# Transposing a long-convolution filter by halves, so that its first transform step shares the row-tiled code of the other inputs

## The chip, the cores and the metric

One core of one Trainium2 chip. The metric is the device time of one execution, in microseconds. The kernel before: 1922.31 us, median of 3 runs (1921.58 to 1922.76).

## The reference, cut to what matters

The reference is a forward pass and its gradients, for one sequence of 2048 steps of 1024 channels. It adds a gated MLP (three weight matrices of 1024 x 3584, with their gradients) to a convolution branch:

```python
kv = k_shift * v                                   # 4-tap shift of k, times v
y  = irfft(rfft(kv_pad) * rfft(ssm_k_pad))[:S]     # long convolution, one filter per channel
y  = q * (y + kv * ssm_D)
out = x + y + MLP(layernorm(x))                    # and the gradients of all inputs but B_x
```

`ssm_k`, the filter, has shape (channels, time); every other input of the convolution has shape (time, channels). So the filter alone must be transposed before it is transformed.

## The kernel before

The MLP's large matmuls keep TensorE busy. The convolution, in 8 groups of 128 channels, is cut into small steps; each is issued after 8 or 16 large matmuls. `hn` is one group's filter, 128 channels x 2048 time steps. Sixteen whole transposes turn it into `hT`. In each of them the filter's columns are the weights: they are loaded into TensorE first (`PEld`, `LDWEIGHTS <-hn` in the profile), and an identity matrix of 128 columns is then streamed past them (`MATMUL pst<-ident,hn`). With time written as 32 q' + 16 u + r, row 2q' + u of `hT` holds the steps with that q' and u: even rows are u = 0, odd rows u = 1.

```python
def h_tile(self, st):
    hT = self.ttile("hT")
    hv = st["hn"][:].rearrange("p r c -> p (r c)").rearrange("p (q r) -> p r q", r=16)
    pst = self.ps.tile([P, 16, P], BF16, name="pst", tag="aps")
    for r in range(16):
        self.pri.now()
        self.pri.pin(self.nc.tensor.transpose(pst[:, r, :], hv[:, r, :], self.identA[:]))
    self.act(hT[:, 0:16, :], pst[:])
    return hT
```

The first step of the filter's transform needs the rows of one u only. The table `RH` therefore has two versions, each zero in the rows of the other u, and the step makes four passes of two 128-row matmuls:

```python
def fwd1_filter(self, st, hT):
    B = st["Bh"] = self.big.tile([P, 64, NB1, 2], BF16, name="B", tag="big")
    for r0 in range(0, NB1, 8):
        ps = self.ps.tile([P, 1024], F32, name="ps0", tag="aps")
        for jj in range(2):
            r = r0 % 16 + 4 * jj
            self.mm(ps[:, 512 * jj:512 * jj + 512], self.RH[:, r0 // 16].rearrange("p e a l -> p (e a l)"),
                    hT[:, r:r + 4, :].rearrange("p r c -> p (r c)"))
        self.act(B[:, :, r0:r0 + 8, :], ps[:].rearrange("p (r cp i) -> p cp r i", r=8, i=2))
        yield
```

The other inputs are loaded with u = 0 on partitions 0 to 63 and u = 1 on 64 to 127. Their first step uses 64-row matmuls, two at a time on the two halves of TensorE's rows:

```python
def fwd1(self, st, key, src):
    ...
            ps = self.ps.tile([P, 2, 4, P], F32, name="ps1", tag="aps")
            for u in range(2):
                rows = slice(64 * u, 64 * u + 64)
                self.mm(ps[:, u].rearrange("p r c -> p (r c)"), self.R[rows].rearrange("p e a l -> p (e a l)"),
                        src[rows, j:j + 4, :].rearrange("p r c -> p (r c)"))
    ...
```

## Time and profile before

| | before |
|---|---|
| time, median of 3 | 1922.31 us |
| span of the profiled run | 1918.5 us |
| TensorE busy | 1909.4 us |
| VectorE, ScalarE busy | 47%, 33% of the span |
| filter transposes, per group, from the end of the block before to the next block | 1.01 us |
| first step of the filter, per group | 4 x 0.431 = 1.72 us |

TensorE is busy nearly without a gap. A step of the convolution branch thus costs what it delays the large matmul behind it, and this is read in the timeline from start to start, not from the durations. TensorE's waits (engine, tile, line, what it waited for; total us, times, longest):

```profile
PE ps_g L805 <- DMA wg<-in_B_W_gate_dram: 1.6, 1, 1.6
PE ps_warm L851 <- POOL warm L848: 1.5, 1, 1.5
PE ps_g L805 <- DVE xnT L839: 1.0, 2, 0.7
```

All of them lie in the first 104 us of 1918.

### The profile page before, as it was taken

How to read it: one execution, taken by the hardware profiler on the slowest of the kernel's cores; microseconds unless marked ns; L12 is line 12 of the kernel's file. 1: busy time of each engine (PE TensorE's matmuls, PEld its weight loads, DVE VectorE, ACT ScalarE, POOL GpSimd, SP SyncE). 2: the span in 40 equal slices, each digit the busy share in tenths (PEclk: the TensorE clock that was granted, in tenths of full speed). 3: DMA queues.
4: the chain of work that ended last, by engine and by line, in shares of the span. 5: the costliest groups of instructions: out<-in, count | busy, mean ns of one | idle time of the engine just before them, and what ended most of it. 6: DMA issues, size and time to landing. Idle time of an engine off the chain costs nothing.

```text
span 1918.5 us, 36320 instructions
## 1 busy us (share of the span) xinstructions
PE 1909.4 (100%) x15582; PEld 886.9 (46%) x15582; DVE 910.2 (47%) x1364; ACT 635.8 (33%) x867; POOL 15.7 (1%) x38
## 2 busy tenths in 40 slices
PE   9999999999999999999999999999999999999999
PEld 4444444444444444444444444444444544444444
DVE  6767767767777754534444354310122232222222
ACT  5854354364364354354344344321000000000000
POOL 1100000000000000000000000000000000000000
PEclk9999999999999999999999999999999999999999
DMA  9975778974874982645663633385999964554553
GB/s 249 276 179 144 178 185 183 221 189 133 186 187 134 248 225 78 175 128 183 158 163 92 170 100 122 100 203 209 257 240 254 235 157 121 121 121 121 121 121 72
DMA packets 628002, 323.16 MB, mean 168 GB/s; under 512 B 458360, under 2 KB 597376, under 8 KB 627840
## 3 DMA queue, kind: packets, MB, share of 16 engines
q1 hardware_dynamic: 617344, 299.99, 64.1%
q10 hardware_dynamic: 9216, 16.65, 2.9%
q0 software_dynamic: 1280, 4.20, 0.7%
q8 instruction: 122, 2.00, 0.4%
q14 instruction: 40, 0.33, 0.1%
HBM read 143.79 MB, written 95.44 MB: 125 GB/s over the span
## 4 chain that ended last, share of the span: by engine, by line
PE 96%; DVE 1%; ACT 1%; DMA 1%; issue 0%; POOL 0%; SPq 0%; ACTq 0%; POOLq 0%
PE ps_x L1283 20%; PE ps_w L1056 20%; PE ps_o L1214 10%; PE ps_h L805 9%; PE ps_u L805 9%; PE ps_g L805 9%; PE ps_d L1056 9%; PE ps L72 7%; PE ps_d L1069 1%; PE ps_w L1069 1%; ACT ln_j L743 1%; PE ps_warm L851 0%; PE pst L308 0%; PE ps_r L1244 0%; DMA wg<-in_B_W_gate_dram 0%
## 5 line engine op out<-in xcount | busy, mean ns | idle before, releaser
L1056 PE MATMUL ps_w<-ugs,xn_nat 128*128 128x512 bf16 x1728 | 383.9, 379 | 0.0
L805 PEld LDWEIGHTS <-xnT 128*128 128x128 bf16 x1792 | 170.2, 98 | 212.0 <-issue 10.2
L1056 PEld LDWEIGHTS <-xn_nat 128*128 128x128 bf16 x1728 | 164.9, 98 | 199.4 <-issue 5.5
L805 PE MATMUL ps_g<-wg,xnT 128*128 128x512 bf16 x896 | 207.0, 379 | 3.2 <-DMA wg<-in_B_W_gate_dram 1.6
L1301 ACT ACTIVATE w<-xn,m 128x512 f32<-128x512 bf16 x32 | 24.3, 806 | 553.0 <-issue 317.2
L805 PE MATMUL ps_u<-wu,xnT 128*128 128x512 bf16 x896 | 207.0, 379 | 0.5 <-ACT gh L975 0.4
L805 PE MATMUL ps_h<-wdT,goT 128*128 128x512 bf16 x896 | 206.1, 379 | 0.0
L1283 PE MATMUL ps_x<-wgT,ggT 128*128 128x512 bf16 x896 | 198.6, 379 | 0.0
L1283 PE MATMUL ps_x<-wuT,guT 128*128 128x512 bf16 x896 | 198.6, 379 | 0.0
L1214 PE MATMUL ps_o<-wd,hT 128*128 128x512 bf16 (+1 forms) x896 | 187.6, 372 | 0.0
L1056 PE MATMUL ps_d<-g_nat,hs 128*128 128x512 bf16 x768 | 172.1, 379 | 0.0
L1283 PEld LDWEIGHTS <-guT 128*128 128x128 bf16 x896 | 87.7, 98 | 105.7
L1283 PEld LDWEIGHTS <-ggT 128*128 128x128 bf16 x896 | 87.7, 98 | 105.5
L1214 PEld LDWEIGHTS <-hT 128*128 128x128 bf16 x896 | 87.7, 98 | 99.9
L805 PEld LDWEIGHTS <-goT 128*128 128x128 bf16 x896 | 85.2, 98 | 102.6 <-issue 2.9
L319 DVE STREAM_TRANSPOSE flp<-C 128x1024 f32<-128x1024 f32 x48 | 90.5, 1930 | 83.4 <-ACT C L76 83.4
L908 DVE SCALAR_TENSOR_TENSOR ru<-ru,ps_u 128x512 bf16<-128x512 bf16 x112 | 76.5, 683 | 108.6 <-issue 43.3
L975 ACT CAST gh<-ps_h 128x512 bf16<-128x512 f32 x112 | 65.4, 585 | 164.1 <-PE ps_h L805 154.8
L1160 ACT CAST wi<-ps_w 128x512 bf16<-128x512 f32 x108 | 63.6, 589 | 161.8 <-PE ps_w L1056 150.1
L76 ACT CAST C<-ps 128x1024 bf16<-128x1024 f32 x96 | 92.5, 1015 | 69.1 <-PE ps L72 68.1
L319 DVE STREAM_TRANSPOSE flp<-B 128x1024 f32<-128x1024 f32 x48 | 90.8, 1939 | 48.6 <-ACT B L76 48.6
L1056 PEld LDWEIGHTS <-hs 128*128 128x128 bf16 x768 | 72.7, 98 | 88.9 <-issue 4.2
(175 smaller groups left out, 1482.6 us busy)
## 6 DMA issues: line engine op xcount, KB each, us to landing
ug_d<-ru SPq DMA_DIRECT2D x112, 256.0 KB, 3.6
ugs<-ug_d SPq DMA_DIRECT2D x112, 256.0 KB, 4.4
wg<-in_B_W_gate_dram SPq DMA_DIRECT2D x56, 256.0 KB, 4.7
wu<-in_B_W_up_dram SPq DMA_DIRECT2D x56, 256.0 KB, 4.8
h_d<-ht SPq DMA_DIRECT2D x112, 128.0 KB, 3.6
hs<-h_d SPq DMA_DIRECT2D x56, 256.0 KB, 5.1
out_dram<-wi SPq DMA_DIRECT2D x56, 256.0 KB, 2.5
gt<-in_grad_out_dram SPq DMA_DIRECT2D x32, 256.0 KB, 4.0
```

What stands on the lines that cost most here:

```text
L72: self.pri.pin(self.nc.tensor.matmul(out, lhsT=lhsT, rhs=rhs, start=start, stop=stop))
L76: self.pri.pin(self.nc.scalar.copy(out=out, in_=in_))
L319: self.pri.pin(self.nc.vector.transpose(out=df[:, c0:c0 + 32, :], in_=sf[:, c0:c0 + 32, :]))
L805: self.pri.pin(self.nc.tensor.matmul(ps[:], lhsT=xT[:, kt * P:(kt + 1) * P], rhs=w(kt), start=(kt == 0), stop=(kt == self.DT - 1)), always ...
L908: self.pri.pin(nc.vector.scalar_tensor_tensor(out=ru[s][:, 1, :], in0=ru[s][:, 0, :], scalar=0.0, in1=ps[:], op0=ALU.is_gt, op1=ALU.mult))
L975: self.pri.pin(nc.scalar.copy(out=gh[:], in_=ps[:]))
L1056: self.pri.pin(self.nc.tensor.matmul(ps[:], lhsT=lhsT(st), rhs=rhs(st), start=(st == 0), stop=(st == self.ST - 1)))
L1069: self.pri.pin(self.nc.tensor.matmul(ps[i][:], lhsT=lhsT(i, st), rhs=rhs(i, st), start=(st == 0), stop=(st == self.ST - 1)))
L1160: self.pri.pin(nc.scalar.copy(out=wo[0][:, d, :], in_=ps[:]))
L1214: nc.tensor.matmul(ps, lhsT=hT[:, kt, :], rhs=self.wd[:, kt, oc], start=(kt == 0), stop=(kt == self.FT - 1))
L1283: nc.tensor.matmul(ps, lhsT=T[:, kt, :], rhs=W[:, kt, oc], start=(i == 0), stop=(i == n - 1))
L1301: nc.scalar.activation(out=w[:, oc], in_=xn[:, oc], func=ACT.Identity, scale=m[:, 7:8], bias=m[:, 6:7])
```

## The change

The intent: put the filter on partitions in the layout of the other inputs (u = 0 below, u = 1 above), so that it can use their row-tiled first step. That step needs half the passes, and the zero-padded tables go. The price is 32 transposes of 64 columns in place of 16 of 128. (The removal of `RH` and of the two index vectors for it from the tables is cut here.)

```diff
     def h_tile(self, st):
         hT = self.ttile("hT")
-        hv = st["hn"][:].rearrange("p r c -> p (r c)").rearrange("p (q r) -> p r q", r=16)
+        hv = st["hn"][:].rearrange("p r c -> p (r c)").rearrange("p (q u r) -> p u r q", u=2, r=16)
         pst = self.ps.tile([P, 16, P], BF16, name="pst", tag="aps")
         for r in range(16):
-            self.pri.now()
-            self.pri.pin(self.nc.tensor.transpose(pst[:, r, :], hv[:, r, :], self.identA[:]))
+            for u in range(2):
+                self.pri.now()
+                self.pri.pin(self.nc.tensor.transpose(pst[64 * u:64 * u + 64, r, :], hv[:, u, r, :], self.identA[:]))
         self.act(hT[:, 0:16, :], pst[:])
...
-    def fwd1_filter(self, st, hT):
-        ...
...
-        f1h = self.fwd1_filter(st, hT)
+        f1h = self.fwd1(st, "Bh", hT)
         f1g = self.fwd1(st, "Bg", gt)
         yield f1h, (lambda: self.gate_grad(st)) if gi == 0 else None
-        yield f1h, tk
-        yield f1h, self.both(lambda: self.add_D(st), tk)
+        yield None, tk
         yield f1h, tk
         yield None, tk
-        flH = self.flip(st, "fH", st["Bh"][:])
+        yield None, self.both(lambda: self.add_D(st), tk)
+        flH = self.flip(st, "fH", st["Bh"][:].rearrange("p cp u r i -> p cp (u r) i"))
```

More of the change, by code (lines that the diff above doesn't have):

```diff
@@ L122, in tables @@
         self.R = con.tile([P, 2, 2, NB1], BF16, name="R")
-        self.RH = con.tile([P, 2, 2, 2, NB1], BF16, name="RH")
         self.RB = con.tile([P, 64], BF16, name="RB")
@@ L147, in tables @@
         n1 = pbit(63, 1.0, "n1p")
-        n1h = pbit(126, 0.5, "n1h")
-        up = pbit(1, 1.0, "up")
         def first(n, name):
@@ L160, in first @@
             return tr
-        tr = first(n1h, "H")
-        nup = lin(up, -1.0, 1.0, "nup")
-        for u, mu in ((0, nup), (1, up)):
-            V.tensor_scalar(out=self.RH[:, u], in0=tr[:], scalar1=mu[:], scalar2=None, op0=ALU.mult)
         tr = first(n1, "R")
@@ L320, in flip @@
             yield
-    def fwd1_filter(self, st, hT):
-        B = st["Bh"] = self.big.tile([P, 64, NB1, 2], BF16, name="B", tag="big")
-        for r0 in range(0, NB1, 8):
-            ps = self.ps.tile([P, 1024], F32, name="ps0", tag="aps")
-            for jj in range(2):
-                r = r0 % 16 + 4 * jj
-                self.mm(ps[:, 512 * jj:512 * jj + 512], self.RH[:, r0 // 16].rearrange("p e a l -> p (e a l)"),
-                        hT[:, r:r + 4, :].rearrange("p r c -> p (r c)"))
-            self.act(B[:, :, r0:r0 + 8, :], ps[:].rearrange("p (r cp i) -> p cp r i", r=8, i=2))
-            yield
     def add_D(self, st):
         for rows in (slice(0, 32), slice(64, 96)):
-            b0 = st["Bh"][rows, :, 0, :]
+            b0 = st["Bh"][rows, :, 0, 0, :]
             self.tt(b0, b0, st["sD"][rows].rearrange("p (cp i) -> p cp i", i=2), ALU.add)
```

## The prediction

> **What bounds the kernel now.** I read the page's busy shares and its chain first, then the sum of TensorE's waits, then the timeline of TensorE around the places that change.
>
> ```profile
> span 1918.5 us, 36320 instructions
> PE 1909.4 (100%) x15582; PEld 886.9 (46%) x15582; DVE 910.2 (47%) x1364; ACT 635.8 (33%) x867; POOL 15.7 (1%) x38
> PE 96%; DVE 1%; ACT 1%; DMA 1%; issue 0%; POOL 0%; SPq 0%; ACTq 0%; POOLq 0%
> ```
>
> TensorE is busy for 1909.4 of 1918.5 us and holds 96% of the chain that ends last. Its waits in the whole run come to 5.0 us (1.6 for a weight DMA, 1.5 at the start, the rest under 1). No other engine passes half. So the span is, nearly one for one, the sum of how long each step holds TensorE, and what the change is worth is the change of that sum. Busy figures of a group cannot be used for it: a record lasts longer than the time after which the next may start (a 512-column matmul is shown with 379 ns, yet 64 of them take 13.83 us from the first start to the start of what follows, 216 ns each). I therefore count from start to start.
>
> The convolution branch is fed to TensorE in small steps between blocks of 8 or 16 large matmuls. Timeline of TensorE at the end of one channel group and the start of the next (start, duration, instruction):
>
> ```profile
> 234.75 1.17 PE L308 MATMUL pst<-ident,hn 128*128 128x128 bf16 x16
> 235.76 1.89 PE L805 MATMUL ps_g<-wg,xnT 128*128 128x512 bf16 x8
> ...
> 245.33 0.59 PE L72 MATMUL ps<-hT,RH 128*128 128x512 bf16 x2
> 245.76 1.89 PE L805 MATMUL ps_h<-wdT,goT 128*128 128x512 bf16 x8
> 247.49 0.59 PE L72 MATMUL ps<-hT,RH 128*128 128x512 bf16 x2
> 247.92 1.89 PE L805 MATMUL ps_g<-wg,xnT 128*128 128x512 bf16 x8
> ...
> 252.24 3.62 PE L805 MATMUL ps_u<-wu,xnT 128*128 128x512 bf16 x16
> 255.79 0.61 PE L72 MATMUL ps<-gt,R 64*128 64x512 bf16 x4
> 256.32 3.63 PE L805 MATMUL ps_h<-wdT,goT 128*128 128x512 bf16 x16
> ```
>
> Line 308 is the filter's transpose, RH its zero-padded first step, and `gt,R` the first step of another input, which already is what the filter's will become. No line shows an idle gap: each step simply adds its length to the kernel.
>
> **What the Trainium skill says.** (1) "TensorEngine Tiling (Array Packing)", Key Properties: row or column tiles work independently, and changing the tiling mode drains the engine. The trace agrees: the four 64-row matmuls of `gt,R` start in two pairs, 0.54 us in all where four whole passes would take 0.86, and there is about 0.1 us lost before them and 0.1 after. (2) "TensorE: Matmul & The Clock Gate", Weight-path perf modes: the fast weight load needs 128 weights; the transposes fall to 64. The trace agrees that there is a difference: contiguous loads of 128 columns take 98 ns, those of 64 columns (RB) 110. (3) "SBUF — State Buffer", Door 1: lines of 16 bytes, and each access that crosses into a new line pays a penalty. The filter's weights are read with a step of 16 elements (32 bytes), so every element is on a new line; the change makes the step 32, again one line each. The trace shows the penalty:
>
> ```profile
> L308 PEld LDWEIGHTS <-hn x128: 142/148/164, 94.0 to 1116.4; 128*128 128x128 bf16 x128
> L837 PEld LDWEIGHTS <-ln_x x64: 95/98/98, 9.4 to 41.9; 128*128 128x128 bf16 x64
> ```
>
> The same transpose with contiguous weights (second line) loads in 98 ns and repeats every 56 ns; the strided one loads in 148 and repeats every 63 (1.01 us over 16), so here the load, not the matmul, sets the pace. (4) "PSUM — Partial Sum Buffer", PSUM bank collisions: two row tiles must not write one bank at the same time. The code that the filter now shares gives each half its own bank, so no wait comes of that.
>
> **The change part by part.**
>
> *First step of the filter.* Removed, per group: four steps of two matmuls, 245.76 − 245.33 = 0.43 us each (twice 216 ns, no drain), so 1.72 us. Added: two steps of four 64-row matmuls. From the timeline: the block before starts at 252.24 and holds 16 x 0.216 = 3.46 us, so it is through at 255.70; what follows the step starts at 256.32; the step costs 0.62 us. Two make 1.24. (A group at 1133 us, in the other phase of the kernel, gives 0.62 too.) Gain 0.48 us per group, 8 groups: 3.8 us. A naive count, eight passes made four, would be 0.86 per group; the entry into the tiled mode and the way out eat nearly half.
>
> *Transposes.* Removed per group: 16 of 128 columns, 235.76 − 234.75 = 1.01 us. Added: 32 of 64 columns, in pairs into the two halves of the partitions. Each still streams the 128-column identity. If the two of a pair run together, the floor is 16 pairs x 56 ns = 0.90 us, plus entry and exit of the mode. The nearest relative in the trace is the tap sums:
>
> ```profile
> 192.97 3.62 PE L805 MATMUL ps_u<-wu,xnT 128*128 128x512 bf16 x16
> 196.52 1.08 PE L72 MATMUL ps<-kp,gks 128*32 128x128 bf16 x64
> 197.53 3.63 PE L805 MATMUL ps_h<-wdT,goT 128*128 128x512 bf16 x16
> ```
>
> 64 matmuls with 32 weight columns each: the same number of weight columns (2048), and the same 16 rounds of 128 columns. The block before is through at 196.43, so the step costs 1.10 us: 0.90 and 0.20 of mode change. With contiguous weights I would thus write +0.1 us per group. With strided ones I have three readings of the 63 ns: if all reads of a partition share one rate (128 in 63 ns), a pair still reads 128 elements, costs 63 ns, and the step 16 x 0.063 + 0.2 = 1.2 us (+0.2 per group, +1.6 in all); if the strided load is now only an ordinary one without the fast mode, 64 columns are under the matmul's 56 ns and the step is 1.1 us (+0.8 in all); if the 63 ns belong to four streams of 32 elements side by side, a 64-column load in one stream takes twice that, 126 ns, and the step is 16 x 0.126 + 0.2 = 2.2 us (+1.2 per group, +9.7 in all). I hold the first two together at about 60%.
>
> *Evictions.* ScalarE's casts into B take 1006 to 1032 ns in both layouts (96 of them, one median of 1013), and there are four per group before and after; the copy of hT stays one of 1.87 us. Two casts now follow each other as they do for `gt`, where no wait of TensorE appears. The step counter of the branch advances equally often, so the interleaving stays.
>
> *Tables.* RH goes: on VectorE two casts of 0.28 us, three index steps and a few one-column instructions, on ScalarE one 0.40 us sine, all near 63 to 68 us. TensorE waits for none of them, so 0, with perhaps 0.4 us either way because ScalarE's order near 92 us, where one 0.4 us wait stands, can change.
>
> *Group 0.* Its third filter step is followed by the 1.6 us weight wait. What is gained or lost before that wait may partly be swallowed: 0.3 us at most, left out.
>
> *Sum.* −3.8 + 0.8 to 1.6 = −2 to −3 us in the likely case, −3.8 + 9.7 = +6 in the bad one.
>
> **The rivals.** (a) *The transposes give it all back* (the third reading above): for it speaks that the strided load already sets the pace, and that without the fast mode fewer streams may read; against it, that halving the columns halves the reads of each load, and that the four tiles of the tap sums load side by side without hurting. It makes about 1928 us. If also the two halves of a pair took turns, 32 x 0.126 + 0.2 = 4.2 us per group, +26 − 3.8: about 1944, still within 2%. (b) *The naive gain*: eight passes become four at full worth and nothing is lost on the transposes, −6.9 us, 1915 us. The 0.62 us of the existing step speaks against it. (c) *A new wait for evictions*: two PSUM tiles of a step must be emptied, about 2 us of ScalarE, before the branch's next use of them. The empty slot after each filter step leaves 3.5 us, and `gt` shows no wait with the same spacing, so 0; if it were to come, under 1 us per group and 8 in all. (d) *VectorE*: adding D moves two slots later, nearer to the flip of B. VectorE has gaps of over 1 us there, and TensorE's next use of the flip lies more than 4 us behind it. 0.
>
> **How the range and the chances follow.** Before is 1922.3 (1921.6 to 1922.8). The likely case gives 1919.5 to 1920.3, the bad one 1928.3. Weighing these at 60 and 30%, with the rest for the turns-taking and the naive cases, I set the middle at 1921 us, a little above the likely case, and the range at 1918 to 1930, which holds both main cases. A change of over 2% would need 38 us, that is 4.8 us per group on steps that now last 1.01 + 1.72 us. Faster: under 1%. Slower: 1%, if the strided loads without the fast mode are much worse than all readings here. Within 2%: 98%.
>
> **What would show each step right or wrong.** The filter's first step should appear as two steps of four 64-row matmuls, 0.60 to 0.65 us from the end of the block before to the start of the one after. The transposes should appear as 32 instructions with 64 weight columns; their step, 1.1 to 1.2 us if I am right, 2.2 if rival (a) is, and the weight load of hn near 110 to 150 ns or near 210. The sum of TensorE's waits should stay near 5 us. I am wrong if the span moves without these steps moving, if the transposes' step passes 1.5 us, or if a new waiting line of TensorE for a B or hT eviction appears.

## The result, and the profile after

| | before | changed |
|---|---|---|
| time, median of 4 runs each | 1921.94 us (1919.28 to 1922.76) | 1922.08 us (1921.57 to 1923.71) |
| span of the profiled run | 1918.5 us | 1919.8 us |
| transposes, per group | 1.01 us | 2.02 us |
| first step of the filter, per group | 1.72 us | 2 x 0.633 = 1.27 us |

The ratio is 1.0005, 95% interval 0.9987 to 1.0022: the same time. Here and below, a ratio is the mean time of one kernel's fast runs over that of the other's of the same rounds, so it is not quite the ratio of the medians quoted. "Us by the ratio" means the ratio minus one, times the median of before.

The page of the changed kernel, its head and the chain that ended last:

```profile
span 1919.8 us, 36326 instructions
PE 1891.6 (99%) x15472; PEld 886.3 (46%) x15710; DVE 908.9 (47%) x1354; ACT 633.6 (33%) x865; POOL 14.9 (1%) x37
PE 97%; issue 1%; DMA 1%; DVE 1%; ACT 0%; SPq 0%; DVEq 0%; ACTq 0%
```

TensorE's busy time seems to have fallen by 18 us. It has not: this trace has 15710 weight loads but only 15472 matmuls, so 238 matmul records are missing, and the page shows the holes as "issue". I read the timeline from a second profile of the same kernel (experiment 6), which has all 15710. End of one group and start of the next (start, duration, instruction):

```profile
230.55 3.62 PE L788 MATMUL ps_h<-wdT,goT 128*128 128x512 bf16 x16
234.09 2.00 PE L302 MATMUL pst<-ident,hn 128*64 128x128 bf16 x32
236.02 1.90 PE L788 MATMUL ps_g<-wg,xnT 128*128 128x512 bf16 x8
...
243.87 1.89 PE L788 MATMUL ps_h<-wdT,goT 128*128 128x512 bf16 x8
245.70 0.60 PE L72 MATMUL ps<-hT,R 64*128 64x512 bf16 x4
246.23 1.90 PE L788 MATMUL ps_h<-wdT,goT 128*128 128x512 bf16 x8
247.97 1.89 PE L788 MATMUL ps_g<-wg,xnT 128*128 128x512 bf16 x8
249.79 0.60 PE L72 MATMUL ps<-hT,R 64*128 64x512 bf16 x4
250.33 1.90 PE L788 MATMUL ps_g<-wg,xnT 128*128 128x512 bf16 x8
```

The 16 large matmuls from 230.55 hold TensorE for 16 x 0.216 = 3.46 us, to 234.01; the next block starts at 236.02. So the transposes cost 2.01 us. The block of 8 from 243.87 is through at 245.60, and the next starts at 246.23: 0.63 us for half of the first step. Over all groups the medians are 2.02 and 0.633 us.

The first line explains the transposes, in the same profile (durations in ns: least, median, most):

```profile
L302 PEld LDWEIGHTS <-hn x256: 185/204/209, 94.7 to 1120.1; 128*64 128x64 bf16 x128
L302 PE MATMUL pst<-ident,hn x256: 273/274/323, 94.8 to 1120.2; 128*64 128x128 bf16 x128
```

Half as many columns, and the load takes longer than the whole one of before (204 ns against 148). In the trace the two loads of a pair start 4 ns apart and the pairs repeat every 111 ns; a whole transpose repeated every 63 to 64. Per group the change gives back 1.724 - 1.266 = 0.46 us and takes 2.02 - 1.01 = 1.01: a loss of 0.55 us, 4.4 us in 8 groups. The timed runs show less than that. The experiments are about both points: why the halves are slow, and where the rest of the loss is.

### The profile page after: what moved, and what is told of

It is laid out like the page before. It is cut to its first block, busy times and chain, and to the rows that moved or that the text cites. A ratio compares the mean times of both kernels' runs of the same rounds, so it can differ in the third digit from the quotient of the medians.

```text
span 1919.8 us, 36326 instructions
## 1 busy us (share of the span) xinstructions
PE 1891.6 (99%) x15472; PEld 886.3 (46%) x15710; DVE 908.9 (47%) x1354; ACT 633.6 (33%) x865; POOL 14.9 (1%) x37
## 3 DMA queue, kind: packets, MB, share of 16 engines
q8 instruction: 123, 2.02, 0.4%
## 4 chain that ended last, share of the span: by engine, by line
PE 97%; issue 1%; DMA 1%; DVE 1%; ACT 0%; SPq 0%; DVEq 0%; ACTq 0%
PE ps_x L1266 20%; PE ps_w L1039 19%; PE ps_h L788 10%; PE ps_g L788 10%; PE ps_u L788 10%; PE ps_o L1197 10%; PE ps_d L1039 9%; PE ps L72 6%; PE ps_d L1052 1%; PE pst L302 1%; DMA ugs<-ug_d 0%; PE ps_w L1052 0%; PE ps_r L1227 0%; DMA wg<-in_B_W_gate_dram 0%; ACT ln_j L726 0%
## 5 line engine op out<-in xcount | busy, mean ns | idle before, releaser
L1039 PE MATMUL ps_w<-ugs,xn_nat 128*128 128x512 bf16 x1670 | 375.6, 380 | 5.8 <-issue 4.1
L788 PE MATMUL ps_h<-wdT,goT 128*128 128x512 bf16 x862 | 201.8, 380 | 3.0 <-issue 1.8
L1039 PE MATMUL ps_d<-g_nat,hs 128*128 128x512 bf16 x740 | 167.4, 380 | 3.2 <-issue 2.5
```

The lines of the kernel that those rows point to most:

```text
L788: self.pri.pin(self.nc.tensor.matmul(ps[:], lhsT=xT[:, kt * P:(kt + 1) * P], rhs=w(kt), start=(kt == 0), stop=(kt == self.DT - 1)), always ...
L1039: self.pri.pin(self.nc.tensor.matmul(ps[:], lhsT=lhsT(st), rhs=rhs(st), start=(st == 0), stop=(st == self.ST - 1)))
```

## The experiments

Three calls, each on one chip, each with its own runs of the kernel before. A line "before" below is the median of those.

### 1. The new first step alone

The changed kernel with the whole transposes put back. The rows of `hT` are then in the wrong order for `R`, so the result is wrong; work and waits are those of the right one.

```diff
-        hv = ....rearrange("p (q u r) -> p u r q", u=2, r=16)
+        hv = ....rearrange("p (q r) -> p r q", r=16)
-            for u in range(2): transpose(pst[64 * u:64 * u + 64, r, :], hv[:, u, r, :], ...)
+            transpose(pst[:, r, :], hv[:, r, :], ...)
```

> The changed kernel with the 16 whole transposes of before put back (rows in the wrong order, so a wrong result on purpose). Theory (the two parts simply add on TensorE: the first step gains 0.48 us per group, the transposes lose 1.0): 1.01 us for the transposes, two steps of 0.62 us, so 8 x 0.48 = 3.8 us under the kernel before, about 1918. Rival (the first step's gain is lost elsewhere, for instance in later waits): within 1 us of before although the steps measure 0.62.

Measured: 1916.02 us (5 runs) against 1921.35; ratio 0.9973 (0.9960 to 0.9985), so 5.2 us less by the ratio. The transposes' step is 1.00 us and the first step's two halves 0.634 each. The first part of the change is a gain and it reaches the end of the kernel; it isn't lost in later waits. The interval holds the expected 3.8 us (it reaches from 2.9 to 7.7), the middle lies 1.4 us beyond it (more on that under 5, 6 and 7).

### 2. Half transposes of neighbouring columns

Same instructions, but each weight load reads 64 neighbouring elements (wrong result).

```diff
-        hv = ....rearrange("p (q u r) -> p u r q", u=2, r=16)
+        hv = ....rearrange("p (u r q) -> p u r q", u=2, r=16)
```

> The changed kernel, its 32 half transposes reading 64 neighbouring columns instead of every 32nd (wrong result on purpose; the count and shape of instructions are the same). Theory (each weight load is one stream that pays for every new line): the load falls from 204 to about 110 ns, a pair repeats every 56 ns and not 111, the transposes' step falls from 2.03 to about 1.1 us. Rival (column tiling with two tiles is itself slow, loads can't hide behind the matmul of their own tile): it stays at 2.0 us.

Measured, weight load and step in its profile:

```profile
L302 PEld LDWEIGHTS <-hn x256: 106/110/110, 94.2 to 1112.9; 128*64 128x64 bf16 x128
```

```profile
229.99 3.62 PE L788 MATMUL ps_h<-wdT,goT 128*128 128x512 bf16 x16
233.53 1.08 PE L302 MATMUL pst<-ident,hn 128*64 128x128 bf16 x32
234.55 1.90 PE L788 MATMUL ps_g<-wg,xnT 128*128 128x512 bf16 x8
```

The load falls to 110 ns; the step is 234.55 - (229.99 + 3.46) = 1.10 us. So column tiling in halves (two transposes side by side, each on one half of TensorE's columns) is not slow: 16 rounds of 56 ns and 0.2 us for going into the tiled mode and out. The distance between the elements read is what costs. One run took 1916.49 us.

### 3. Quarters

The changed kernel with 64 transposes of 32 columns, in four column tiles; the result is right.

```diff
-            for u in range(2):
-                transpose(pst[64 * u:64 * u + 64, r, :], hv[:, u, r, :], ...)
+            for u in range(2):
+                for w in range(2):
+                    b = 64 * u + 32 * w
+                    transpose(pst[b:b + 32, r, :], hv[:, u, r, 32 * w:32 * w + 32], ...)
```

> The changed kernel with 64 quarter transposes of 32 columns each (right result). Theory (64 elements in a stream at 1.7 ns each set the 111 ns; four streams of 32 run side by side): a round of four repeats every 56 to 63 ns, the step takes 1.1 to 1.25 us in place of 2.03, 6 to 7 us under the changed kernel in all and 2 to 3 under before. Rival (the two column tiles share one rate of reads, about 0.87 ns per element): a round of four still reads 128 elements in 111 ns, 2.0 us, no gain. Rival (cost per instruction): 64 instructions, 4 us.

```profile
L304 PEld LDWEIGHTS <-hn x512: 132/143/158, 94.4 to 1115.4; 128*32 128x32 bf16 x171
```

The step is 1.22 us, and in the trace a round of four starts every 59 to 62 ns. Twice the instructions, and much less time: four loads side by side each pay for 32 elements, where two each paid for 64. That agrees with the reading of one stream per load, each with its own pace: 111 ns / 64 = 1.7 ns for each far element in halves, 60 / 32 = 1.9 in quarters, and 63 / 32 = 2.0 for the whole load of before, if that reads in four chunks of 32 side by side, as the Trainium skill has it for the fast load ("TensorE: Matmul & The Clock Gate", Weight-path perf modes). A common rate of reads for the whole partition is out: 128 far elements per round took 111 ns in halves and 59 to 62 in quarters. Time: 1918.23 us against 1921.35, ratio 0.9982 (0.9970 to 0.9995), 3.5 us less by the ratio, where 2 to 3 were expected. So this version beats the kernel before, which the change itself does not.

### 4. The halves alone, in the kernel before

The whole transposes of before cut into halves, with the old step of 16 elements and the old first step; the result is right.

```diff
-            transpose(pst[:, r, :], hv[:, r, :], ...)
+            for u in range(2):
+                transpose(pst[64 * u:64 * u + 64, r, :], hv[:, r, 64 * u:64 * u + 64], ...)
```

> The kernel before with its 16 whole transposes cut into 32 halves, read with the old step of 16 elements (right result, old zero-padded first step). Theory (any step beyond one line costs the same): the transposes' step is 2.0 us as in the changed kernel, 8 x 1.0 = 8 us over before, about 1930. Rival (it is the step of 32 elements, not the half loads, that is slow): 1.1 to 1.2 us, 1 to 2 us over before.

```profile
L309 PEld LDWEIGHTS <-hn x256: 194/218/223, 93.0 to 1122.6; 128*64 128x64 bf16 x128
```

The step is 2.19 us, a little more than with a distance of 32, and in the trace the pairs repeat every 121 ns, about twice the 63 to 64 of the whole transposes at the same distance. So it isn't the change of the distance from 16 to 32 that made the load slow, it is the load of 64 far elements in one stream. Time: 1927.43 us against 1921.35, ratio 1.0033 (1.0020 to 1.0047), 6.3 us more by the ratio; 8 x 1.17 = 9.4 was to come by the steps.

### 5, 6 and 7. How much can be told apart, and the tables

The kernel before against itself (no edit), the changed kernel again (no edit), and the changed kernel with the table `RH` built as before and not used:

```diff
...
+        tr = first(n1h, "H")
+        nup = lin(up, -1.0, 1.0, "nup")
+        for u, mu in ((0, nup), (1, up)):
+            V.tensor_scalar(out=self.RH[:, u], in0=tr[:], scalar1=mu[:], scalar2=None, op0=ALU.mult)
```

> The kernel before, unchanged, against itself. It measures how far two sets of runs of one kernel differ and whether the first 110 us of its one profile (where all other profiles are 1 to 3 us ahead of it) is typical. Theory (those microseconds are the luck of one profile): this profile reaches 110 us 1 to 2 us earlier than the first one did, and the ratio is within 0.1% of 1. Rival (a real cost of the kernel before in its first 110 us): the same positions as in the first profile, to 0.3 us.

> The changed kernel, unchanged, timed with more rounds. Step sum on TensorE: 2 x 0.633 in place of 4 x 0.431 (-3.7 us in 8 groups) and 2.02 in place of 1.02 us (+8.1 us), so +4.4 us, less what the weight wait of group 0 swallows (up to 1.6): 3 to 4.4 us over before. Rival (a gain elsewhere, of 3 to 4 us, that cancels it): within 1 us of before.

> The changed kernel with the table RH built as before and not used (right result). If leaving out the table work is what gains 2 to 3 us in the first 110 us: 2 to 3 us over the changed kernel. If TensorE never waited for it, as I predicted: within 1 us of the changed kernel of the same call.

| | median of 5 | ratio to before (1923.14 us, 1919.30 to 1924.33) |
|---|---|---|
| 5, before again | 1921.22 us | 0.9995 (0.9983 to 1.0008) |
| 6, changed again | 1922.75 us | 1.0004 (0.9992 to 1.0017) |
| 7, changed with tables | 1923.27 us | 1.0007 (0.9993 to 1.0020) |

Two sets of runs of one kernel differ by 0.05% here, about 1 us, and the single runs of before are spread over 5 us. Against set 5 the changed kernel is 1.5 us slower, against the other set 0.4 faster by the medians. Keeping the tables costs 0.5 us by the medians and is not told apart from nothing. Experiment 6 thus missed what I expected of it: 3 to 4.4 us over before by the steps, and 0.8 by the ratio, where its rival had "within 1 us". Its interval (1.5 us under to 3.3 over) excludes neither the lower end of the one nor the other.

To see where the spread sits, I worked out from each trace when the same large weight load starts, the 481st of the MLP, some 20 us after group 0's filter, and how long it is from there to the last one:

| trace | the 481st load starts | from there to the last |
|---|---|---|
| before, and again | 129.4, 128.1 us | 1779.0, 1780.1 us |
| changed, again, with tables | 126.8, 128.5, 130.9 | 1782.9, 1783.4, 1783.0 |
| 1, new step alone | 128.1 | 1777.2 |
| 4, halves alone | 127.9 | 1786.9 |

From 130 us on, the traces say what the steps say. Seven groups at 0.55 us make 3.9 us; the three traces of the changed kernel are 3.5 us above the two of before. Seven at 1.17 make 8.2; experiment 4 shows 7.4. In the first 130 us, traces of one and the same kernel differ by over 1 us (the second one of before is 1.3 us earlier than the first, the three of the changed kernel are spread over 4), much more than the 0.55 us that group 0 should add. Part of group 0's change can moreover be swallowed there by a wait for weights. TensorE in the first trace of before:

```profile
101.70 0.59 PE L72 MATMUL ps<-hT,RH 128*128 128x512 bf16 x2
103.91 2.79 PE L805 MATMUL ps_g<-wg,xnT 128*128 128x512 bf16 x8 [1.61 <-DMA wg<-in_B_W_gate_dram]
106.53 0.59 PE L72 MATMUL ps<-hT,RH 128*128 128x512 bf16 x2
```

and in the trace of experiment 6:

```profile
102.80 0.60 PE L72 MATMUL ps<-hT,R 64*128 64x512 bf16 x4
103.34 0.60 PE L788 MATMUL ps_g<-wg,xnT 128*128 128x512 bf16 x2
104.12 2.25 PE L788 MATMUL ps_g<-wg,xnT 128*128 128x512 bf16 x7 [0.18 <-DMA wg<-in_B_W_gate_dram]
```

Here the changed kernel comes to the weights a microsecond later and finds them there: its wait is 0.2 us in place of 1.6. In its first trace the wait is 0.5 us, but in that of experiment 7 it is 2.2, longer than before: the traces don't reach this point at the same time, so what is swallowed differs from one to the next. The last line of before's trace shows one thing more: its fourth filter step still stands behind this wait, and the changed kernel has none there. Where both wait for the same weights, group 0 therefore doesn't lose 0.55 us but gains some 0.43. That is an estimate from the lines above, and a sum for the changed kernel is then 3.9 - 0.4 = 3.4 us in place of 4.4.

What stays open: the timed ratios put the changed kernel 0.8 to 1.0 us over before, with intervals that end at 3.3 and 4.2 us; the part after 130 us accounts for 3.5. The difference of some 2.5 us is of the size of the scatter of the first 130 us. The other variants lie on the same side of their step sums (1.4 us in experiment 1, and in experiment 4 some 2 of the 8.2 us of seven groups; about 1.5 in experiments 3 and 9), so a constant part of it may be real. It need not belong to the change: the kernel before against itself lies on that side too, by 1.0 us in experiment 5, within its interval. The tables aren't shown to be its cause: experiment 4 has them and shows it too.

### 8. The order made by a copy

If far elements are the cost, they can be read elsewhere. ScalarE copies the filter once per group into the order in which the transposes want it, into the buffer of `ksh`, which is free then; 16 whole transposes then read neighbours. The copy is issued 15 steps of the branch ahead, and for group 0 ahead of the transposes by what the program counts as 4.5 us of large matmuls. (One whole transpose that reads u and q as two dimensions would need no copy. It did not build.)

```diff
...
+    def h_order(self, st):
+        hq = st["hq"] = self.lng.tile([P, 16, P], BF16, name="hq", tag="ksh")
+        hv = st["hn"][:].rearrange("p r c -> p (r c)").rearrange("p (q u r) -> p r u q", u=2, r=16)
+        self.act(hq[:].rearrange("p r (u q) -> p r u q", u=2), hv)
...
-            for u in range(2): transpose(pst[64 * u:64 * u + 64, r, :], hv[:, u, r, :], ...)
+            transpose(pst[:, r, :], st["hq"][:, r, :], ...)
```

> The changed kernel, its filter first put in order by one copy per group on ScalarE (into a buffer that is free then), so that 16 whole transposes read 128 neighbouring columns (right result). Theory (the pace of the transposes is the lines that their weight loads touch; the change's gain is in its first step alone): load 98 ns, one transpose each 56 ns, step 0.90 us; per group 0.46 + 0.12 us under before, 8 x 0.58 = 4.6 us, about 1917. Rival (the copies on ScalarE delay evictions that TensorE waits for): the steps measure so, but waits of TensorE eat it, 1920 or more.

Measured: 1928.63 us against 1923.14, ratio 1.0036 (1.0024 to 1.0049). Slower, as the rival said (a copy delays an eviction, that is the emptying of TensorE's results by ScalarE, for which TensorE waits), but by one wait in group 0 alone. ScalarE in its timeline:

```profile
78.43 3.61 ACT L76 COPY hq<-hn 128x2048 bf16<-128x2048 bf16 x1 [9.27 <-DMA hn<-in_A_ssm_k_dram]
```

and TensorE's longest wait:

```profile
PE ps_u L797 <- ACT gh L967: 10.2, 1, 10.2
```

The copy of group 0 stood at the head of ScalarE's queue from 69 us, 9.3 us before its data were there and much earlier than 4.5 us ahead of the transposes, and nothing behind it ran in that time: the next eviction (`gh`, for which TensorE waited) started at 81.94 us. TensorE lost 10.2 us once. The transposes themselves did as expected, with a step of 0.90 us. An edit of mine, not the idea, was wrong.

### 9. The copy, but not in group 0

Group 0 uses the quarters of experiment 3, groups 1 to 7 the copy; the result is right. The edit, shortened, against experiment 8:

```diff
-        yield 4500
-        self.h_order(nx)
-        yield 4500
+        yield 9000
...
+            if "hq" in st: transpose(pst[:, r, :], st["hq"][:, r, :], ...)       # groups 1 to 7
+            else: four quarters as in experiment 3                               # group 0
```

> The kernel with the ordering copy, but group 0 transposed in quarters without a copy (the copy of group 0 had blocked ScalarE for 9.3 us behind the load of hn); right result. Theory: no ACT wait of 10 us is left; groups 1 to 7 take 0.90 us for the transposes and 1.27 for the first step, 0.58 under before each; with what group 0 keeps after its weight wait (0.4), 4 to 5 us under before: about 1917, and 1 to 2 under the quarters alone. Rival (the copy of 3.7 us on ScalarE makes new waits of TensorE in the groups too): no better than the quarters.

Measured: 1915.27 us (5 runs, 1914.66 to 1916.64) against 1921.21; ratio 0.9970 (0.9956 to 0.9983), 5.8 us less by the ratio, where 4 to 5 were expected. One group's transposes in its profile:

```profile
231.08 3.62 PE L802 MATMUL ps_h<-wdT,goT 128*128 128x512 bf16 x15
234.53 1.06 PE L307 MATMUL pst<-ident,hq 128*128 128x128 bf16 x16
235.42 1.89 PE L802 MATMUL ps_g<-wg,xnT 128*128 128x512 bf16 x8
```

235.42 - 234.53 = 0.89 us, with no loss on entry, since no tiled mode is entered (one of the 16 matmul records before is missing). The copies take 3.78 us of ScalarE each, seven of them, and no wait of TensorE comes of it: its waits are those of the start and holes of missing records. From the 481st load to the last it is 1775.6 us, 4.0 under before; seven times 0.46 + 0.12 is 4.0. By its steps this is the fastest correct version (0.89 us against 1.22 for the transposes of a group); by the timed ratios its interval overlaps that of the quarters, which are the simpler version.

### 10 and 11. How far is far

The changed kernel, its half transposes reading every 8th and every 4th element (wrong results):

```diff
-        hv = ....rearrange("p (q u r) -> p u r q", u=2, r=16)
+        hv = ....rearrange("p (a q b) -> p a b q", q=64, b=8)     # experiment 11: b=4
...      (the index of hv in the transposes changes with it)
```

> The changed kernel, half transposes reading every 8th element (16 bytes; wrong result on purpose). If the cost is one new 16-byte line per element: as at a step of 16 or 32, load about 204 ns, step 2.0 us. If it grows with the distance: in between, 150 ns.

> The changed kernel, half transposes reading every 4th element (8 bytes, two to a line of 16; wrong result on purpose). If two reads in a line are enough for the full rate: as with neighbouring columns, load 110 ns, step 1.1 us. If only neighbours are read at the full rate: 150 to 204 ns, 1.5 to 2.0 us.

Weight loads of experiment 10, then of experiment 11:

```profile
L302 PEld LDWEIGHTS <-hn x256: 192/217/218, 93.9 to 1119.7; 128*64 128x64 bf16 x128
```

```profile
L302 PEld LDWEIGHTS <-hn x256: 135/143/159, 93.6 to 1113.5; 128*64 128x64 bf16 x128
```

| distance of the elements read | 1 | 4 | 8 | 16 | 32 |
|---|---|---|---|---|---|
| load of 64 columns, ns | 110 | 143 | 217 | 218 | 204 |
| transposes' step, us | 1.11 | 1.21 | 2.16 | 2.19 | 2.02 |

The cost rises until the distance is 8 elements, 16 bytes, and no further at 16 and 32 elements (distances between 4 and 8 weren't tried). That is what the 16-byte lines of the Trainium skill ("SBUF — State Buffer", Door 1) lead one to expect, now seen in weight loads. With two elements to a line the load still takes 33 ns more than with neighbours, so my "as with neighbouring columns" was not quite met, but the matmul's own 56 ns hide most of it. Single runs: 1923.42 and 1917.04 us.

## Why the prediction was right or wrong

Right in the range (1918 to 1930; 1922.08 came), and 1.1 us from the middle. But the step that I held likely failed, and that the middle came so near was luck: the transposes cost some 7 us more than the likely case had, and the timed kernel came out 3.4 to 3.6 us below the sum of its measured steps. By the steps alone the kernel would have come to about 1926 us, and the range holds that only because it was made to hold rival (a) too.

- **What bounds the kernel**: right. TensorE stays busy throughout, and from 130 us on the span follows the sum of its steps to about 1 us.
- **First step of the filter**: right. Predicted two steps of 0.62 us, measured 0.633; gain 0.46 us per group where 0.48 stood; experiment 1 shows that the gain reaches the end.
- **Transposes**: wrong in the choice. "I hold the first two together at about 60%", with a step of 1.1 to 1.2 us; it was 2.02. The third reading, which I gave as rival (a), held: one stream per load. Its size was 10% high (2.2 us, as I doubled the whole load's 63 ns to 126; pairs repeat every 111). At the distance of 16 from which the 63 were read the doubling is nearly right: in experiment 4 pairs repeat every 121 ns and the step is 2.19 us. Why a distance of 32 is somewhat cheaper stays open. What I had against it, that halving the columns halves the reads of each load, argued wrongly: a half is read in one stream, and 64 in one stream are more than 32 in each of four, if the fast load of 128 columns reads in four. The tap sums, which I took as the nearest relative, read neighbours in four loads (97 ns each in the profile before), so their 1.10 us could not speak for far elements in two. Experiment 2 (neighbours: 1.10 us) and experiment 3 (quarters: 1.22) decided it.
- **The sum**: with the measured steps it is -3.7 + 8.1 = +4.4 us, where rival (a) had +6. The timed runs show 0.8 to 1.0. Group 0's part can be lost in the start, as the line on group 0 half said; "0.3 us at most" was too low (the wait shrank by 1.1 and 1.4 us in two traces of the changed kernel and grew in the third). About 2.5 us are not accounted for and lie within the scatter of the first 130 us. (A slip in the recorded sum: 1922.3 less 2.2 to 3.0 is 1919.3 to 1920.1, not 1919.5 to 1920.3.)
- **Rival (b)**, the naive 6.9 us: out, the tiled mode costs 0.2 us per visit. **(c)** and **(d)**, new waits for evictions or VectorE: none came; the casts into B stayed at 1.02 us (1.01 before), as predicted.
- **Tables**: right as far as the runs can tell (0.5 us between medians of 5).
- **The marks set beforehand** worked: "if the transposes' step passes 1.5 us" was named as the sign of error, and it is what the trace shows, with the load "near 210" (204).

## What to carry to other kernels

A transpose can be paced by its weight load when the weights are read at a distance: here the identity's 128 columns took 56 ns, and half loads of far elements 111 to 121. Count the elements that one load must fetch; here four narrow loads or one whole load were better than two half ones, and a copy on an engine with time to spare that made the order first was best in the steps. (Matmuls that stream 512 columns were not tried with far weights.) Keep such a copy away from the head of a queue whose data have not arrived: one waiting instruction cost 10 us. Read the steps beside the clock: two parts of a change, here 3.7 us gained and about 8 lost, can look like nothing, and the half that gains can be kept with another way of making the order (experiments 3 and 9).

## What the Trainium skill lacked or had wrong

- "SBUF — State Buffer", Door 1, says that one can stride for free up to 8 bf16 elements. In weight loads of 64 columns a distance of 8 costs as much as 16 or 32 (217, 218 and 204 ns), and 4 is not free either (143 against 110).
- "TensorE: Matmul & The Clock Gate", Weight-path perf modes, gives the fast weight load's pattern as packed or strided, without a cost for strided. Whole loads of 128 columns took 98 ns packed and 148 at a distance of 16; without the fast mode, 64 columns at that distance took 218.
- "TensorEngine Tiling (Array Packing)", Key Properties, says that a change of mode drains the engine but not what that costs: about 0.2 us for entry and exit together (0.633 us for a step whose passes take 0.43; 1.11 for one of 0.90).
- No page that I read gives the pace of weight loads in column tiles whose elements lie apart: 128 elements at a distance of 32 took 111 ns in two loads and 59 to 62 in four.
